# Reads of the states as whole-array matmuls, a choice matrix in one step, and a new planned order, in a fused attention and mixture-of-depths kernel

## The chip, the cores and the metric

The kernel runs on one core of one Trainium2 chip. The metric is the device time of a run in microseconds (us). A core has a matmul engine (TensorE, PE in the profile), three engines for elementwise work (VectorE or DVE, ScalarE or ACT, GpSimd or POOL), a queue engine (SyncE or SP) and 16 DMA engines. They run side by side and wait for one another by semaphores. Matmuls write to PSUM, from which ACT or DVE copy the results into SBUF.

## The reference

Eight batches of x have 8 heads, 512 rows and 64 columns; each head has a state of 32 rows. Rows read the state and the state reads the rows; the 544 results of a batch are then rows of 512 columns, of which the 128 with the highest gate score go through two layers.

```python
# attention, per batch and head; scale = 1/8
a     = softmax(scale * x @ state.T)          # 512 x 32
xread = a @ state                             # 512 x 64
a2    = softmax(scale * state @ x.T)          # 32 x 512
sread = a2 @ x                                # 32 x 64
y = concat([xread, sread], axis=rows)         # heads side by side: 544 x 512 per batch
# mixture of depths, per batch
scores = y @ w_gate                           # 544
top = indices of the 128 largest scores
h = relu(y[top] @ w1)                         # 128 x 1024
y[top] += sigmoid(scores[top])[:, None] * (h @ w2)
```

All numbers are float32.

## The kernel before

**Tiling.** The 8 heads of a batch are two groups g of four heads q; 4 x 32 states fill the 128 partitions. The 512 rows are four chunks c of 128. Per batch, in the program's order:

- `turn` (L340): 16 transposes of x on PE, in four pairs of heads, each pair copied by ACT (L349; two pairs of batch 0 by DVE, L347) into a buffer of the ring `xT`.
- `scores` (L369): scores in PSUM (`ps_s`), states by rows.
- The row softmax: DVE turns the scores in 32x32 blocks (`in`, L383), takes the largest (L387), subtracts (L390); ACT takes exp (L393); DVE sums (L397), scales (L402) and turns back (`out`, L405) into `eT`.
- The state softmax: largest by DVE (`smax`, L411), exp by ACT into `a` (`s_exp`, L415).
- `read` (L447): for each chunk, `eT` times the states `st_v` into the PSUM tile `ps_o`, of which there is one. ACT copies the rows to `xs` (`rows`, L451); DVE sums the gate parts (`gate`, L455).
- `turn_a` (L469), copied by ACT (L472), and `state_read` or sread (L485): the other softmax is transposed and multiplied by x. DVE scales the result (L490).
- The stores of `xs` (L512) and of the states' rows (L517) on the SP queue.

**The states for a read.** `st_v` has, for each batch and group, 128 partitions (head and state) and 2 x 64 + 1 columns: two heads in blocks on a diagonal, for each half of the partitions, and one column with the state's share of the gate score. A read is therefore four matmuls, two groups by two halves. `pool_states` zeroes the tile (L224) and copies the blocks (L218) on POOL; DVE fills the last column (`state_gates`, L229 and L231); `twice` doubles the states for PE's transposes of them (`state_T`, L314), on DVE or POOL (L221).

**The choice.** The gate scores are spread over all partitions by transposes (`row`, L558 and L561), DVE counts for each row how many are larger (`win`, L577), PE adds up those that were chosen before it (`over`, L604), DVE makes the offsets (L610, L611) and from them a 0/1 matrix `oh`, with five instructions (`one_hot`, L617). PE picks the row numbers with it (L632), and POOL fetches the chosen rows back from the output by an indirect DMA (L524) into the ring `xr`.

**The layers** (`layers`) take the chosen rows of the groups of batches [0], [1, 2], [3, 4], [5, 6] and [7]: transposes (`xg`, L690), first layer (L707) of 256 or 128 columns, relu by ACT (L711), second layer (L724), gate and sum by DVE (L727), and an indirect DMA that puts the rows back (L524).

**Buffers.** A `Ring` has a fixed number of buffers; a piece that takes one waits until the users of the old content are done. The ring of x has five buffers, one of which first holds the states. PSUM has two tiles `ps_tr` for every transpose and small result, one `ps_s`, one `ps_o` and two `ps_h`.

**Order.** Nothing above runs in the program's order. Each step is added as a piece with an engine, a planned length, the pieces that it follows, and the buffers that it takes and uses. `carry_out` then plays a clock: it takes the engine whose next piece can start first, and among its pieces that can start within `SOON[engine]` of that time the one with the smallest key. The key is the batch number plus `LATER[name]`. That order is then emitted, and each engine works its own list strictly in it:

```python
t, e = min(((at, p.engine) for at, p in ready), key=lambda r: r[0])
at, p = min(((at, p) for at, p in ready if p.engine == e and at <= t + SOON[e]), key=lambda r: r[1].key)
```

Of the kernel before, what the change touches and what calls it, by code (L numbers as in the profile page):

```python
# [18 lines left out]
def kernel(  # L19
# [35 lines left out]
    def pool(name, bufs, **kw):  # L55
        return ctx.enter_context(tc.tile_pool(name=name, bufs=bufs, **kw))

    N_X, N_XR = 5, 8
    const = pool("const", 1)
    xin = pool("xin", N_X)  # L60
    work = pool("work", 1)
# [5 lines left out]


    HOP = 0.1
    SOON = {"PE": 0.0000, "DVE": 0.4931, "ACT": 0.0000, "POOL": 1.8045, "SP": 0.3000}  # L70

    LATER = {
        "add": -100.0000, "below": 1.9500, "exp": -0.0600, "exps": -0.7084, "fetch": 0.2600, "first": 100.0000,
        "gate": -0.5600, "gate_s": 4.8280, "heads": 0.4872, "in": -1.0433, "index": -2.8646, "load": -50.0000,
        "load_x": -2.0000, "max": 4.0896, "mult": 4.3959, "numbers": 0.2545, "off": -1.9260, "oh": -2.4538,
        "out": 3.4200, "over": -2.2366, "parts": -2.6851, "pick": 0.3200, "put": -100.0000, "read": 4.9387,
        "relu": -100.0000, "row": -4.7962, "row_kept": 4.8694, "row_s": -3.1695, "row_s_kept": -0.1742,
        "rows": 5.0000, "score_s": -3.7680, "scores": -1.0816, "second": 100.0000, "sexp": -0.1370,
        "sigmoid": 0.2238, "smax": 1.1888, "sread": 1.2957, "srows": -2.7199, "ssum": 1.4281, "state_T": 0.3300,
        "state_gates": 2.6509, "states": -1.3434, "store": 4.7700, "sub": -1.8119, "sum": -4.7918,  # L80
        "tables": -4.6345, "turn": -0.1899, "turn_a": 4.0218, "turned": 4.7352, "turned_a": -5.0000,
        "twice": -2.9080, "win": 4.2491, "xg": 90.0000, "xg_kept": -100.0000,
    }
    class Buf:

# [26 lines left out]
    def carry_out():  # L112

        free, taken, done, end, order = {}, {R_X: [stb], stb: True}, {}, {}, []
        left = list(pieces)

        def since(p, q):
            return end[q] + HOP if q.engine != p.engine else done[q]

        while left:  # L120
            ready = []
            for p in left:
                if any(q not in end for q in p.after) or any(buf not in taken for buf in p.uses):
# [12 lines left out]
            assert ready, "the plan cannot go on"  # L136
            t, e = min(((at, p.engine) for at, p in ready), key=lambda r: r[0])
            at, p = min(((at, p) for at, p in ready if p.engine == e and at <= t + SOON[e]), key=lambda r: r[1].key)
            for buf in p.takes:
                taken[buf.ring].append(buf)  # L140
                taken[buf] = True
            free[e] = done[p] = at + p.length
            end[p] = done[p] + p.lands
            order.append(p)
            left.remove(p)
        for p in order:
            for buf in p.takes:
                buf.ring.take(buf)
            p.fn()
# [6 lines left out]
    P_O = Ring("ps_o", [128, 1024], F32, 1, psum)  # L156
    P_H = Ring("ps_h", [128, 512], F32, 2, psum)
    R_X = Ring("xf", [128, H, NC, D], F32, N_X, xin)
    R_XT = sbuf("xT", [128, 2, 2, 128], 12)
    R_E = sbuf("e", [128, 32, Ns], 2)  # L160
    R_A = sbuf("a", [128, 2, 2, 256], 1)
    R_ET = sbuf("eT", [128, 2, 2, 2, 128], 2)
    R_AT = sbuf("aT", [128, NC, 128], 2)
    R_XS = sbuf("xs", [128, NC, Dm], 2)
    R_ROW = sbuf("srow", [128, SP], 1)
    R_WIN = [sbuf(f"win{c}", [128, SP - first[c]], 1, BF16) for c in range(NC + 1)]
    R_OH = sbuf("oh", [128, NC + 1, n_slots], 1, BF16)
# [26 lines left out]
                                                          ap=[[D, 4], [0, Ns], [1, D]]))  # L194

    ident = const.tile([128, 128], F32, name="ident")
    st_v = const.tile([128, B, 2, 2 * D + 1], F32, name="st_v")
    wg_s = const.tile([128, 2, D], F32, name="wg_s")
    after = const.tile([128, SP], F32, name="after")
    places = const.tile([128, NC + 1, n_slots], F32, name="places")  # L200
# [26 lines left out]
    def state_gates(lo, hi):  # L227
        t = work.tile([128, hi - lo, 2, D], F32, name="state_g", tag="hT", bufs=1)
        nc.vector.tensor_tensor(out=t, in0=st_c[:, lo:hi, :, 0],  # L229
                                in1=wg_s.unsqueeze(1).to_broadcast([128, hi - lo, 2, D]), op=ALU.mult)  # L230
        nc.vector.reduce_sum(out=st_v[:, lo:hi, :, 2 * D], in_=t, axis=AX.X)  # L231

    def pool_tables():

# [8 lines left out]


        nc.gpsimd.memset(sc, 0.0)

    def row_numbers():

# [77 lines left out]
    def attention(b):  # L326
# [6 lines left out]
        for pair in range(H // 2):  # L333
# [10 lines left out]
            def keep(ps=ps, t=t, on=on):  # L344
# [92 lines left out]
        for c in range(NC):  # L437
            o = Buf(P_O)

            def view(o):  # L440
                return o.ap.rearrange("p (i g m) -> p i g m", i=2, g=2)

            def read(c=c, o=o):
                for g in range(2):
                    for i in range(2):
                        half = slice(D * i, D * (i + 1))
                        nc.tensor.matmul(view(o)[:, i, g, 0:2 * D + 1], eT.ap[half, c % 2, g, c // 2], st_v[half, b, g],  # L447
                                         start=True, stop=True)

            def keep(c=c, o=o):  # L450
                nc.scalar.copy(out=xs.ap[:, c].rearrange("p (g i m) -> p g i m", g=2, i=2),  # L451
                               in_=view(o)[:, :, :, 0:2 * D].rearrange("p i g m -> p g i m"))

            def gate(c=c, o=o):
                nc.vector.tensor_reduce(out=sc[:, b, c:c + 1], in_=view(o)[:, :, :, 2 * D], axis=AX.XY, op=ALU.add)  # L455

            p = add("PE", 0.66, read, after=[p_eT, p_pool[b], p_sg[b]], takes=[o], uses=[eT],
                    key=key("read"))
            p_sc.append(add("DVE", 0.15, gate, after=[p, p_tab], uses=[o], key=key("gate")))
            p_xs.append(add("ACT", 0.6, keep, after=[p], takes=[] if c else [xs], uses=[o] + ([xs] if c else []), key=key("rows")))  # L460

        aT, p_aT = [], []
        for g in range(2):
# [10 lines left out]
            p = add("PE", 0.5, turn, after=[p_a[g]], takes=[ps, t], uses=[a], key=key("turn_a"))  # L474
# [54 lines left out]
    def choice(b, tmp, p_sc, p_xt, p_st1):  # L529
# [33 lines left out]
        p = add("PE", 0.55, row_x, after=p_sc, takes=[ps1], key=key("row"))  # L563
        p_r1 = add("ACT", 0.59, lambda: nc.scalar.copy(out=srow.ap[:, 0:S], in_=ps1.ap), after=[p], takes=[srow],
                   uses=[ps1], key=key("row_kept"))
        p = add("PE", 0.2, row_s, after=[p_ss, p], takes=[ps2], key=key("row_s"))
# [54 lines left out]
        p_oh = add("DVE", 1.06 * n_slots / 128, one_hot, after=[p], takes=[oh], key=key("oh"))  # L621

        units = []
        for lo, hi in slot_tiles:
# [166 lines left out]
```

## Time and profile before

| | us |
|---|---|
| median of 3 runs (lowest to highest) | 221.9 (221.47 to 222.27) |
| time of the profiled execution | 222.47 |
| its span | 220.7 |
| PE busy | 202.4 |
| DVE busy | 124.5 |
| ACT busy | 85.9 |
| POOL busy | 49.9 |

The span runs from the first to the last instruction; a run's time has 1.8 us more around it. An engine's busy time is the union of its instructions. In the tables of groups, a line has the source line, the engine, the operation, output and inputs, the shapes and the count; after the first bar the busy time in us and the mean of one in ns, and after the second the idle time just ahead of them. "64*128" is the part of the matmul array that an instruction uses, rows by columns; 128*128 is the whole. In the timeline, a line has the start and the length in us, the engine, the line and the count, and in brackets what the engine stood idle for. PE's granted clock was 0.999 of full speed over the span.

### The profile page before, as it was taken

To read this page: it belongs to the slowest core of one execution; us is meant where nothing else is said; L and a number is where in the kernel's file an instruction comes from. 1 tells how busy PE (TensorE), PEld (TensorE's weight loads), DVE (VectorE), ACT (ScalarE), POOL (GpSimd) and SP (SyncE) were. 2 spreads that over 40 slices of the span, in tenths; PEclk is the share of its full clock that TensorE was granted. 3 is DMA by queue.
4 is the path that set the end of the run, shared out by engine and by line. 5 is a ranking of instruction groups with operands and counts; after the bars stand their busy time and mean duration, and the time that the engine had idled before them with its cause. 6 is when DMAs were issued, how large, how long until landed. Compare 5 with 4: busy or idle time off the path is not lost.

```text
span 220.7 us, 4784 instructions
## 1 busy us (share of the span) xinstructions
PE 202.4 (92%) x1928; PEld 142.4 (65%) x1928; DVE 124.5 (56%) x349; ACT 85.9 (39%) x172; POOL 49.9 (23%) x128
## 2 busy tenths in 40 slices
PE   2497898898999999999999999999999999999990
PEld 2355675676878954778886455888645788447840
DVE  3159989987887897798868896730062100011001
ACT  3139878778776315453725133323301021100200
POOL 7229001041105124110142423301035200011001
PEclk9999999999999999999999999999999999999999
DMA  6999969826314301150050711502212000010001
GB/s 213 329 306 402 369 207 288 305 54 205 131 74 157 111 0 48 52 196 9 34 207 13 238 50 49 239 3 95 95 48 94 33 19 0 0 50 11 36 0 48
DMA packets 17406, 26.59 MB, mean 120 GB/s; under 512 B 5608, under 2 KB 13800, under 8 KB 16360
## 3 DMA queue, kind: packets, MB, share of 16 engines
q1 hardware_dynamic: 15032, 21.43, 28.0%
q0 software_dynamic: 1280, 4.20, 6.1%
q10 hardware_dynamic: 1072, 0.66, 0.9%
q8 instruction: 15, 0.25, 0.5%
q14 instruction: 7, 0.06, 0.1%
HBM read 15.27 MB, written 11.01 MB: 119 GB/s over the span
## 4 chain that ended last, share of the span: by engine, by line
PE 55%; issue 20%; DMA 8%; POOL 6%; ACT 5%; DVE 2%; POOLq 1%; ACTq 0%
PE ps_h L707 17%; PE ps_h L724 12%; PE ps_o L447 7%; DMA out_dram<-xs 4%; PE ps_tr L340 4%; PE ps_s L369 3%; DMA xf<-in_state_dram 3%; PE ps_tr L469 3%; PE ps_tr L485 3%; ACT a L415 2%; POOL out_dram L524 2%; PE ps_tr L604 2%; PE ps_tr L558 2%; POOL xr L524 1%; ACT xT L349 1%
## 5 line engine op out<-in xcount | busy, mean ns | idle before, releaser
L707 PE MATMUL ps_h<-xg,w 128*128 128x256 f32 (+1 forms) x320 | 60.4, 341 | 0.0
L724 PE MATMUL ps_h<-w,hT 128*128 128x512 f32 x128 | 58.9, 601 | 0.0
L707 PEld LDWEIGHTS ps_h<-xg,w 128*128 128x128 f32 x320 | 50.3, 191 | 5.9 <-issue 0.5
L724 PEld LDWEIGHTS ps_h<-w,hT 128*128 128x128 f32 x128 | 23.1, 190 | 23.2 <-issue 22.5
L340 PE MATMUL ps_tr<-ident,xf 128*128 128x128 f32 x128 | 21.5, 311 | 9.7 <-DMA xf<-in_x_dram 4.1
L727 DVE SCALAR_TENSOR_TENSOR ot<-ps_h,z,xr 128x512 f32<-128x512 f32 x8 | 6.0, 749 | 43.1 <-PE ps_h L724 43.1
L451 ACT COPY xs<-ps_o 128x512 f32<-128x512 f32 x32 | 18.8, 586 | 28.2 <-PE ps_o L447 14.1
L711 ACT ACTIVATE hT<-ps_h 128x512 f32<-128x512 f32 x16 | 9.5, 596 | 49.7 <-PE ps_h L707 49.7
L340 PEld LDWEIGHTS ps_tr<-ident,xf 128*128 128x128 f32 x128 | 15.5, 156 | 14.8 <-issue 5.3
L577 DVE SCALAR_TENSOR_TENSOR win<-srow,sc,after 128x544 bf16<-128x544 f32 (+4 forms) x40 | 18.3, 501 | 8.4 <-ACT srow L567 8.4
L447 PE MATMUL ps_o<-st_v,eT 64*128 64x129 f32 x256 | 22.9, 297 | 0.1
L447 PEld LDWEIGHTS ps_o<-st_v,eT 64*128 64x128 f32 x256 | 16.8, 186 | 6.0 <-issue 2.8
L349 ACT COPY xT<-ps_tr 128x512 f32<-128x512 f32 x30 | 16.8, 589 | 9.6 <-PE ps_tr L340 9.6
L524 POOL DMA_INDIRECT out_dram<-ot,idx x8 | 8.4, 1047 | 53.2 <-DVE ot L727 51.0
L524 POOL DMA_INDIRECT xr<-out_dram,idx x8 | 8.5, 1057 | 48.1 <-DVE idx L637 16.3
L588 POOL CAST aux<-sc 128x5 bf16<-128x5 f32 x8 | 1.9, 232 | 52.3 <-DVE sc L455 38.3
L455 DVE TENSOR_REDUCE sc<-ps_o 128x1 f32<-128x4 f32 x32 | 5.1, 158 | 12.1 <-PE ps_o L447 7.0
L415 ACT ACTIVATE a<-ps_s,nm 128x512 f32<-128x512 f32 x16 | 10.9, 689 | 2.0 <-DVE nm L411 2.0
L383 DVE STREAM_TRANSPOSE e<-ps_s 128x1024 f32<-128x1024 f32 x8 | 10.0, 1247 | 2.9 <-PE ps_s L369 2.9
L369 PE MATMUL ps_s<-xT,st_T 64*32 64x256 f32 x256 | 9.6, 413 | 1.7 <-ACT a L415 1.7
L469 PE MATMUL ps_tr<-ident,a 128*128 128x128 f32 x64 | 10.2, 284 | 1.1 <-ACT a L415 0.5
L397 DVE TENSOR_REDUCE sm<-e 128x32 f32<-128x1024 f32 x8 | 9.7, 1210 | 1.5 <-ACT e L393 1.5
(84 smaller groups left out, 229.9 us busy)
## 6 DMA issues: line engine op xcount, KB each, us to landing
out_dram<-xs SPq DMA_DIRECT2D x8, 1024.0 KB, 4.3
xf<-in_x_dram SPq DMA_DIRECT2D x14, 512.0 KB, 6.8
w<-in_moe_w_dram SPq DMA_DIRECT2D x2, 2048.0 KB, 10.1
xf<-in_x_dram SPq DMA_DIRECT2D x2, 256.0 KB, 3.2
xf<-in_x_dram ACTq DMA_DIRECT2D x2, 256.0 KB
out_dram<-xt SPq DMA_DIRECT2D x32, 16.0 KB, 2.1
xf<-in_state_dram SPq DMA_DIRECT2D x1, 384.0 KB
xf<-in_state_dram ACTq DMA_DIRECT2D x1, 128.0 KB, 7.1
```

What stands on the lines that cost most here:

```text
L340: nc.tensor.transpose(v[:, k, r], xf[b].ap[:, 2 * pair + k, 2 * r:2 * r + 2].rearrange("p w d -> p (w d)"), ident)
L349: nc.scalar.copy(out=t.ap, in_=v)
L369: nc.tensor.matmul(view_s()[Ns * q:Ns * (q + 1), w, g], st_T[half, b, g, Ns * q:Ns * (q + 1)], xT[2 * g + q // 2].ap[half, q % 2].rearrang ...
L383: nc.vector.transpose(out=flat(e), in_=s.ap)
L415: nc.scalar.activation(out=a.ap[:, g], in_=view_s()[:, :, g], func=AF.Exp, bias=tmp["nm"][:, g:g + 1], accum_out=tmp["ss"][:, g:g + 1])
L447: nc.tensor.matmul(view(o)[:, i, g, 0:2 * D + 1], eT.ap[half, c % 2, g, c // 2], st_v[half, b, g], start=True, stop=True)
L451: nc.scalar.copy(out=xs.ap[:, c].rearrange("p (g i m) -> p g i m", g=2, i=2), in_=view(o)[:, :, :, 0:2 * D].rearrange("p i g m -> p g i m"))
L469: nc.tensor.transpose(v[:, c], a.ap[:, g, c % 2, 128 * (c // 2):128 * (c // 2 + 1)], ident)
L524: touches(b, nc.gpsimd.indirect_dma_start(**kw), True)
L577: nc.vector.scalar_tensor_tensor(wins[c].ap[0:n], srow.ap[0:n, f:SP], sc[0:n, b, c:c + 1], after[0:n, 0:SP - f], op0=ALU.is_gt, op1=ALU.mu ...
L707: nc.tensor.matmul(v[:, f, 0:n], w1[:, j, 128 * (f0 + f):128 * (f0 + f + 1)], xg.ap[:, j, 0:n], start=(j == 0), stop=(j == ND - 1))
L724: nc.tensor.matmul(py.ap[0:m], hT.ap[:, f, lo:lo + m], w2[:, f], start=(f == 0), stop=(f == NF - 1))
```

## The change

- `st_v` gets 4 x 64 + 1 columns: all four heads of a group in blocks on one diagonal. A read is two matmuls over all 128 partitions, one for each group, each into a PSUM bank of its own; the copy and the gate sum follow the new layout (two values for four).
- The choice matrix `oh` is made by one tensor_tensor over 5 x 128 columns, with the offsets in two zeroed tiles.
- The rings `xT` and `xr` go from 12 to 8 and from 8 to 6 buffers. `xs` stays at 2 for the capacity of 128.
- In the plan, the turns take their `xT` buffer at the transpose and not at the copy; some planned lengths change; `SOON` and `LATER` have new values, so that every engine's list has another order. If the plan cannot go on, the pieces are emitted in program order; in the build for these shapes they are not.
- The loads' pieces and their keys are the same, and so is their issue up to the weights and batch 4. After that the SP queue has loads and stores in another sequence.

```diff
-    N_X, N_XR = 5, 8
+    N_X, N_XR = 5, 6
+    DV = 4 * D + 1
...
-    SOON = {"PE": 0.0000, "DVE": 0.4931, "ACT": 0.0000, "POOL": 1.8045, "SP": 0.3000}
+    SOON = {"PE": 0.0000, "DVE": 0.5777, "ACT": 0.1173, "POOL": 0.6934, "SP": 0.3000, "DMA": 0.0000}
...
-    R_XT = sbuf("xT", [128, 2, 2, 128], 12)
+    R_XT = sbuf("xT", [128, 2, 2, 128], 8)
...
-    R_XS = sbuf("xs", [128, NC, Dm], 2)
+    R_XS = sbuf("xs", [128, NC, Dm], 2 if cap <= 128 else 1)
...
-    st_v = const.tile([128, B, 2, 2 * D + 1], F32, name="st_v")
+    st_v = const.tile([128, B, 2, DV], F32, name="st_v")
...
+    offs = [const.tile([128, NC + 1], F32, name=f"off{i}") for i in range(2)]
...
         for q in range(4):
-            k = q % 2
             r = slice(Ns * q, Ns * (q + 1))
-            nc.gpsimd.tensor_copy(out=st_v[r, lo:hi, :, D * k:D * (k + 1)], in_=st_c[r, lo:hi, :, 0])
+            nc.gpsimd.tensor_copy(out=st_v[r, lo:hi, :, D * q:D * (q + 1)], in_=st_c[r, lo:hi, :, 0])
...
+        for off in offs:
+            nc.gpsimd.memset(off, 0.0)
...
-            p = add("PE", 0.47 if b else 0.9, turn, after=[px[(pair * len(px)) // (H // 2)]] + last_turn[-1:], takes=[ps], uses=[xf[b]],
+            p = add("PE", 0.62 if b else 0.9, turn, after=[px[(pair * len(px)) // (H // 2)]] + last_turn[-1:], takes=[ps, t], uses=[xf[b]],
                     key=key("turn"))
             last_turn.append(p)
-            p_xT.append(add(on, 0.6, keep, after=[p], takes=[t], uses=[ps], key=key("turned")))
+            p_xT.append(add(on, 0.6, keep, after=[p], uses=[ps, t], key=key("turned")))
...
-        p_s = add("PE", 1.02, scores, after=p_xT + [p_sT[b]], takes=[s], uses=xT, key=key("scores"))
+        p_s = add("PE", 1.09, scores, after=p_xT + [p_sT[b]], takes=[s], uses=xT, key=key("scores"))
...
             def view(o):
-                return o.ap.rearrange("p (i g m) -> p i g m", i=2, g=2)
+                return o.ap.rearrange("p (g m) -> p g m", g=2)[:, :, 0:DV]
 
             def read(c=c, o=o):
                 for g in range(2):
-                    for i in range(2):
-                        half = slice(D * i, D * (i + 1))
-                        nc.tensor.matmul(view(o)[:, i, g, 0:2 * D + 1], eT.ap[half, c % 2, g, c // 2], st_v[half, b, g],
-                                         start=True, stop=True)
+                    nc.tensor.matmul(view(o)[:, g], eT.ap[:, c % 2, g, c // 2], st_v[:, b, g], start=True, stop=True)
...
             def gate(c=c, o=o):
-                nc.vector.tensor_reduce(out=sc[:, b, c:c + 1], in_=view(o)[:, :, :, 2 * D], axis=AX.XY, op=ALU.add)
+                nc.vector.reduce_sum(out=sc[:, b, c:c + 1], in_=view(o)[:, :, 4 * D], axis=AX.X)
...
-            p = add("PE", 0.66, read, after=[p_eT, p_pool[b], p_sg[b]], takes=[o], uses=[eT],
-                    key=key("read"))
+            p = add("PE", 0.46, read, after=[p_eT, p_pool[b], p_sg[b]], takes=[o], uses=[eT], key=key("read"))
...
         def offsets():
-            off = tmp["off"] = small.tile([128, NC + 1], F32, name="off")
+            off = offs[b % 2]
...
         def one_hot():
-            for c in range(NC + 1):
-                m = rows[c]
-                nc.vector.tensor_scalar(oh.ap[0:m, c], places[0:m, c], tmp["off"][0:m, c:c + 1], None, op0=ALU.is_equal)
+            nc.vector.tensor_tensor(out=oh.ap, in0=places, in1=offs[b % 2].unsqueeze(2).to_broadcast([128, NC + 1, n_slots]),
+                                    op=ALU.is_equal)
```

The planned lengths of `turn_a`, `row` and `oh` change as well (to 0.62, 0.62 and 0.82 us), and 50-odd values of `LATER`.

More of the change, by code (lines that the diff above doesn't have):

```diff
@@ L69 @@
     HOP = 0.1
-    SOON = {"PE": 0.0000, "DVE": 0.4931, "ACT": 0.0000, "POOL": 1.8045, "SP": 0.3000}
+    SOON = {"PE": 0.0000, "DVE": 0.5777, "ACT": 0.1173, "POOL": 0.6934, "SP": 0.3000, "DMA": 0.0000}
     LATER = {
[L73 to L82, printed above, removed]
+        "add": -100.0000, "below": 2.0667, "exp": 4.0880, "exps": 0.8708, "fetch": 0.4581, "first": 100.0000,
+        "gate": -5.0000, "gate_s": 5.0000, "heads": 1.5745, "in": 3.4702, "index": -1.4770, "load": -50.0000,
+        "load_x": -2.0000, "max": 0.1851, "mult": 0.6930, "numbers": -1.6286, "oh": 1.8876, "out": 2.4153,
+        "over": 1.7144, "parts": 2.7411, "pick": 0.4214, "put": -100.0000, "read": 5.0000, "relu": -100.0000,
+        "row": 2.2094, "row_kept": 5.0000, "row_s": -0.0444, "row_s_kept": -3.0512, "rows": 3.0716,
+        "score_s": 1.8701, "scores": -0.9593, "second": 100.0000, "sexp": -1.6379, "sigmoid": -2.2897,
+        "smax": -3.4387, "sread": -3.4561, "srows": -3.6081, "ssum": 2.4219, "state_T": -2.7947,
+        "state_gates": 1.5448, "states": -2.8057, "store": 2.3497, "sub": 3.7677, "sum": 1.8368, "tables": 4.1039,
+        "turn": 0.2203, "turn_a": 3.0810, "turned": -4.7340, "turned_a": -4.8726, "twice": 4.7356, "win": -4.4214,
+        "xg": 90.0000, "xg_kept": -100.0000,
     }
@@ L135, in carry_out @@
                     ready.append((at, p))
-            assert ready, "the plan cannot go on"
+            if not ready:
+                order = pieces
+                break
             t, e = min(((at, p.engine) for at, p in ready), key=lambda r: r[0])
@@ L230, in state_gates @@
                                 in1=wg_s.unsqueeze(1).to_broadcast([128, hi - lo, 2, D]), op=ALU.mult)
-        nc.vector.reduce_sum(out=st_v[:, lo:hi, :, 2 * D], in_=t, axis=AX.X)
+        nc.vector.reduce_sum(out=st_v[:, lo:hi, :, 4 * D], in_=t, axis=AX.X)
     def pool_tables():
@@ L440, in view @@
             def view(o):
[L441 removed]
+                return o.ap.rearrange("p (g m) -> p g m", g=2)[:, :, 0:DV]
             def read(c=c, o=o):
                 for g in range(2):
[L445 to L448 removed]
+                    nc.tensor.matmul(view(o)[:, g], eT.ap[:, c % 2, g, c // 2], st_v[:, b, g], start=True, stop=True)
             def keep(c=c, o=o):
[L451 to L452 removed]
+                nc.scalar.copy(out=xs.ap[:, c].rearrange("p (g m) -> p g m", g=2), in_=view(o)[:, :, 0:4 * D])
             def gate(c=c, o=o):
[L455 to L458 removed]
+                nc.vector.reduce_sum(out=sc[:, b, c:c + 1], in_=view(o)[:, :, 4 * D], axis=AX.X)
+            p = add("PE", 0.46, read, after=[p_eT, p_pool[b], p_sg[b]], takes=[o], uses=[eT], key=key("read"))
             p_sc.append(add("DVE", 0.15, gate, after=[p, p_tab], uses=[o], key=key("gate")))
@@ L472, in keep @@
                 nc.scalar.copy(out=t.ap, in_=ps.ap.rearrange("p (c m) -> p c m", c=NC))
-            p = add("PE", 0.5, turn, after=[p_a[g]], takes=[ps, t], uses=[a], key=key("turn_a"))
+            p = add("PE", 0.62, turn, after=[p_a[g]], takes=[ps, t], uses=[a], key=key("turn_a"))
             p_aT.append(add("ACT", 0.59, keep, after=[p], uses=[ps, t], key=key("turned_a")))
@@ L561, in row_s @@
             nc.tensor.transpose(ps2.ap[:, 0:Ns], sc[0:Ns, b, NC:NC + 1].to_broadcast([Ns, 128]), ident[0:Ns, 0:Ns])
-        p = add("PE", 0.55, row_x, after=p_sc, takes=[ps1], key=key("row"))
+        p = add("PE", 0.62, row_x, after=p_sc, takes=[ps1], key=key("row"))
         p_r1 = add("ACT", 0.59, lambda: nc.scalar.copy(out=srow.ap[:, 0:S], in_=ps1.ap), after=[p], takes=[srow],
@@ L614, in one_hot @@
         def one_hot():
-            for c in range(NC + 1):
-                m = rows[c]
-                nc.vector.tensor_scalar(oh.ap[0:m, c], places[0:m, c], tmp["off"][0:m, c:c + 1], None, op0=ALU.is_equal)
+            nc.vector.tensor_tensor(out=oh.ap, in0=places, in1=offs[b % 2].unsqueeze(2).to_broadcast([128, NC + 1, n_slots]),
+                                    op=ALU.is_equal)
         p = add("PE", 0.7, wins_over, after=p_w, takes=[ps3], uses=wins, key=key("over"))
         p = add("DVE", 0.3, offsets, after=[p], uses=[ps3], key=key("off"))
-        p_oh = add("DVE", 1.06 * n_slots / 128, one_hot, after=[p], takes=[oh], key=key("oh"))
+        p_oh = add("DVE", 0.1 + 0.72 * n_slots / 128, one_hot, after=[p], takes=[oh], key=key("oh"))
         units = []
```

## The prediction

> **What bounds the kernel now.** I read the page's busy shares first, then its table of groups split by shape, the stretches, and the matmul engine's timeline.
>
> ```profile
> PE 202.4 (92%) x1928; PEld 142.4 (65%) x1928; DVE 124.5 (56%) x349; ACT 85.9 (39%) x172; POOL 49.9 (23%) x128
> ...
> L447 PE MATMUL ps_o<-st_v,eT 64*128 64x129 f32 x256 | 22.9, 297 | 0.1
> ```
>
> PE is busy for 202 of 220.7 us, and nothing else comes near. The reads (L447) are 22.9 us of that: 32 reads, one per batch and chunk, each of four matmuls; the trace shows 256, since every f32 matmul of this kernel is two instructions there. The stretches say where PE is not full (columns after the two times: PE, PEld, DVE, ACT and POOL busy, clock, DMA):
>
> ```profile
> 0.00:55.50 55.50, 43.41 (x669) 32.01 (x670) 40.73 (x87) 36.41 (x73) 16.66 (x35) 1.00 0.82 266
> 55.50:90.00 34.50, 33.67 (x437) 25.32 (x436) 28.73 (x84) 18.27 (x38) 9.00 (x24) 1.00 0.26 89
> 90.00:152.00 62.00, 61.96 (x557) 44.20 (x557) 46.35 (x147) 23.36 (x47) 13.61 (x42) 1.00 0.26 94
> 152.00:215.30 63.30, 63.30 (x269) 40.91 (x268) 7.96 (x31) 7.81 (x16) 9.52 (x26) 1.00 0.11 42
> ```
>
> Up to 55.5 us (the first matmul of a first layer) PE stands for 12.1 us: 4.07 for the first load, 2.87 behind the state's load, the rest in small waits on copies. From there to 215.3 it stands for under 1 us. So after 55 us each microsecond added to PE's stream is added to the end, and what DVE, ACT or POOL save is worth nothing unless PE waits for it. The price of a PE instruction is the distance between starts, since a matmul's own mean (297 ns) includes a tail that overlaps the next:
>
> ```profile
> 97.05 0.72 PE L447 MATMUL ps_o<-st_v,eT 64*128 64x129 f32 x8
> 97.69 3.72 PE L707 MATMUL ps_h<-xg,w 128*128 128x256 f32 x16
> 101.34 0.72 PE L447 MATMUL ps_o<-st_v,eT 64*128 64x129 f32 x8
> 101.99 1.99 PE L707 MATMUL ps_h<-xg,w 128*128 128x256 f32 x8
> ...
> 173.69 13.98 PE L707 MATMUL ps_h<-xg,w 128*128 128x256 f32 x64
> 187.50 13.90 PE L724 MATMUL ps_h<-w,hT 128*128 128x512 f32 x32
> ```
>
> A read is 97.69 - 97.05 = 0.64 us to the next start; over all reads it is 0.64 or 0.65 whatever stands around it. A 128x256 matmul instruction in a long row is (187.50 - 173.69) / 64 = 0.2158 us. But the sixteen between two reads take 3.65 us where 16 x 0.2158 = 3.45: about 0.1 us is lost at each border with a read. The same comparison over the timeline gives: 0.09 us lost by a whole-array operation ahead of one that uses part of the array, and behind one 0.095 us (layers) or 0.05 us (groups of transposes: 0.49 against 0.44).
>
> **What the Trainium skill says.** "TensorEngine Tiling (Array Packing)", Key Properties, says that changing the tiling mode drains the engine; the trace agrees, with the 0.05 to 0.1 us above. The same section says that tiles work independently; the trace agrees in part: eight instructions of 129 columns, one after the other at the rate of L707, would be 8 x 129/256 x 0.2158 = 0.87 us, two abreast 0.435, and a read takes 0.645. "VectorE: DVE Perf Modes", The perf-mode tier table, has f32 tensor_tensor at a single rate where tensor_scalar runs double; in this trace a tensor_tensor of 768 elements is 0.918 us and one of 256 is 0.42 us, which is 0.97 ns an element.
>
> **The change, part by part.**
>
> 1. Reads. Removed: four matmuls of 64 rows x 129 columns, two abreast. Added: two of 128 rows x 257 columns, so four instructions at 257/256 x 0.2158 = 0.217 us, 0.867 us in all. That is the whole-array form, which L707 shows directly; its weight loads (128x128 f32, four in place of eight) run under the columns there and will here. 0.867 - 0.645 = +0.222 us, times 32 reads: **+7.1 us**, on the path. Bounds for a read: 0.43 if the two matmuls needed one instruction each (no f32 row of the trace does that), 0.97 if it lost a border of its own.
>
> 2. Borders. A read is now whole-array like most of its neighbours. Counted over PE's order in the two programs as built: before, 33 entries into a part-array operation x 0.09 + 22 returns to a layer x 0.095 + 25 returns to transposes x 0.05 = 6.3 us; after, 25 x 0.09 + 22 x 0.095 (15 of them now at a read) + 16 x 0.05 = 5.1 us. **-1.2 us**, on the path. Fourteen reads lose both borders; the rest stand beside small part-array operations that keep theirs.
>
> 3. The choice matrix: five tensor_scalar (1.06 us together in the timeline) become one tensor_tensor of 640 elements, 0.42 + 384 x 0.00097 = 0.79 us. -0.27 us x 8 on DVE, costed at nothing: PE does turns or layers meanwhile. Without that cover it would save at most 2.2 us. The two zeroed offset tiles cost POOL two small memsets (0.1 us each) at its idle start.
>
> 4. Evacuations: L451's copy moves 512 columns as before (0.586 us); the gate reduces two values for four (0.158 us, nearly all fixed). Nothing.
>
> 5. state_V and its memsets: st_v has 257 columns for 129. L224 took 0.52 us for 516 and 1.39 us for 1548 elements, so +0.45 and +1.4 us on POOL. Batch 0 and 1: the memset ends at about 5.5 us, ahead of the state's landing at 8.9; hidden. The rest: POOL now does memset and copies before the doubling (L221), which moves from 16.2 to about 20.6 us. PE needs it at about 28; hidden.
>
> 6. The order. The planner's new weights, read length (0.46) and rings move nearly every row. Smaller rings: xT 12 to 8, so PE turns two batches ahead, not three; xr 8 to 6 never binds (a row set is free when its batch's add is done). xs keeps two buffers here. On SP, store xs of batch 0 now stands ahead of half of load 5 and of load 6: that half is issued at about 37 us instead of before 35, lands (6.8 us median) by 44, and is turned at about 46. The store lands earlier in return. I walked through PE, ACT and DVE in the built order by hand with the durations above, up to the first read of batch 3:
>  - first read of batch 0 at 26.9 us (before 27.85);
>  - first matmul of a first layer at 55.6 (before 55.50), with 164.5 us of PE work left (before 157.4, counted with the same prices, borders included);
>  - first read of batch 3 at 84.7 with 137.2 left: 221.9 in sum; before 80.5 with 132.9 left: 213.4.
> The difference at the last mark is 8.5 us, where parts 1 and 2 make 5.9: PE has stood 2.6 us longer, mainly behind copies of turns that queue on ACT behind exps (36 to 48 us), and behind s_exp of batches 4 and 5 (66 to 80 us). Before pays 0.8 us of such waits afterwards (86 to 89 us), which I assume gone; the walk is rough, so **+2.0 us**, bounded by -1.5 (the small waits could close as well as open) and +5.
>  In the last stretch the fetch of batch 7 has four second-layer and eight first-layer matmuls (6.9 us) ahead of its transposes, and L524 lands 3.5 us after issue; nothing waits. From PE's last matmul to the end stays 5.4 us.
>
> Sum: 7.1 - 1.2 + 2.0 = +7.9 us. The profiled execution has a span of 220.7 and a time of 222.47; 222.47 + 7.9 = 230.4. Its time is 0.57 above the median of the runs, 221.9, so I give **229.8 us**. A difference of 0.3% (0.7 us) is about what a measurement of this kernel can tell from none.
>
> **Rivals.**
>  - *The read becomes cheaper* (the side of faster). If the two matmuls stream once, 2 x 0.217 = 0.434, as the planner's 0.46 supposes: 32 x (0.434 - 0.645) - 1.2 + 2.0 = -6.0, so 215.9 us. The break-even is 0.867 - 7.9/32 = 0.62 us a read. For it: the planner's other lengths are near the trace (turn 0.62, scores 1.09). Against: L707, L724, L369, L485 and L447 all show two instructions per f32 matmul. Chance 0.06.
>  - *The new order starves PE.* DVE is busy for 28.7 of 34.5 us between 55 and 90; with turns only two batches ahead the scores of batch 4 come at about 62 us (before 51), and the chain of seven passes of 1.2 us on DVE decides when a read starts. If PE stood 5 us beyond my walk: 234.8 us. For it: the planner plans with reads of half their length, so its order is meant for another balance. Against: longer reads give DVE more time, not less, and its own work falls by 2.2 us. Chance 0.14.
>  - *The change loses nothing*: borders save more than I count (0.19 at all 32 reads is 6 us) and the small waits close. Then within 0.7 us of before. Against: half the reads stand beside part-array operations. Chance 0.03.
>  - That PE's reads do grow and the order costs about nothing to 5 us: 0.77, from 226 to 233.5.
>
> **How the numbers follow.** The likeliest case gives 229.8. Range 225.8 to 234: from part 6 at about -1.5 with part 2 slightly larger, to part 6 at its upper bound with a little of the starving. Left out: the two good cases and the worst of the starving. Faster 0.06, same 0.03, slower 0.91.
>
> **What would show it.** Right: reads as 128x257, 128 instructions, 0.87 us from start to start; PE busy up by about 6 us; no lost tenth between reads and layers; the one-hot near 0.8 us on DVE. Part 6: first first-layer matmul at 54 to 58 us, PE full from about 85 us to the end. Wrong: a read under 0.62 us, or PE's waits after 55 us above 5 us.

## The result

The changed kernel takes **229.7 us** (median of 4 runs, 229.58 to 230.39) against 222.1 us for the kernel before on the same chip: a ratio of 1.034, interval 1.029 to 1.039. The forecast was 229.8 us. The profiled execution after took 229.67 us with a span of 227.9, where before had 220.7: +7.2.

The page's busy shares after, and its group of the reads:

```profile
PE 207.7 (91%) x1800; PEld 149.2 (65%) x1800; DVE 123.2 (54%) x317; ACT 85.4 (37%) x172; POOL 51.6 (23%) x130
...
L450 PE MATMUL ps_o<-st_v,eT 128*128 128x257 f32 x128 | 35.4, 399 | 2.4 <-ACT xs L453 0.9
```

The read is 128 instructions of 257 columns in place of 256 of 129, and PE's busy time grew by 5.3 us, to 207.7. The rest of the 7.2 is time in which PE stood: 227.9 - 207.7 = 20.2, before 220.7 - 202.4 = 18.3. How the 7.2 splits into work and waits depends in part on the execution that was profiled, as the first experiment shows. The stretches, with the columns as before, say where:

```profile
0.00:55.50 55.50, 42.15 (x599) 31.80 (x600) 38.91 (x80) 33.84 (x67) 17.94 (x37) 1.00 0.85 267
55.50:90.00 34.50, 33.82 (x419) 25.48 (x424) 27.30 (x75) 17.95 (x37) 7.45 (x22) 1.00 0.23 81
90.00:152.00 62.00, 61.12 (x495) 44.66 (x480) 47.06 (x130) 23.97 (x49) 15.70 (x43) 1.00 0.26 97
152.00:222.50 70.50, 70.50 (x304) 47.27 (x302) 9.19 (x34) 9.63 (x19) 9.49 (x26) 1.00 0.10 38
222.50:227.90 5.40, 0.12 (x1) 0.00 (x0) 0.75 (x1) 0.00 (x0) 1.07 (x2) 0.72 0.12 49
```

PE stands 13.35 us in the first stretch (before 12.09), 0.68 in the second (0.83), 0.88 in the third (0.04), and not at all from 152 us to its last matmul. The tail is still 5.4 us. The waits of PE name what it stood for (us in all, times, longest):

```profile
PE ps_tr L345 <- DMA xf<-in_x_dram: 4.4, 1, 4.4
PE ps_tr L319 <- DVE xf L224: 2.9, 1, 2.9
PE ps_tr L345 <- ACT xT L354: 2.2, 4, 1.4
PE ps_o L450 <- ACT xs L453: 0.9, 2, 0.4
...
PE ps_tr L544 <- DVE scr L537: 0.5, 1, 0.5
...
PE ps_o L450 <- DVE sc L456: 0.4, 1, 0.4
```

The first two are loads, as before. The turns' wait for their copies has one of 1.4 us in it, at 18 us. The L450 lines are reads that wait until the one `ps_o` has been copied (L453) or summed (L456). Last, the timeline of PE, where the reads stand between layers:

```profile
105.10 1.14 PE L450 MATMUL ps_o<-st_v,eT 128*128 128x257 f32 x4
106.07 1.89 PE L706 MATMUL ps_h<-xg,w 128*128 128x256 f32 x8
107.80 1.03 PE L450 MATMUL ps_o<-st_v,eT 128*128 128x257 f32 x4
108.67 1.89 PE L706 MATMUL ps_h<-xg,w 128*128 128x256 f32 x8
110.39 1.03 PE L450 MATMUL ps_o<-st_v,eT 128*128 128x257 f32 x4
```

A read behind a layer takes 108.67 - 107.80 = 0.87 us to the next start. The one at 105.10 stands behind a part-array operation, and takes 0.97. Eight layer instructions behind a read take 1.72 or 1.73 us, which is 8 x 0.2158 and no border; before, the same eight took 1.83 to 1.92.

### The profile page after: what moved, and what is told of

Same layout as the page of the kernel before. It is cut to its first block, busy times and chain, and to the rows that moved or that the text cites. A ratio compares the mean times of both kernels' runs of the same rounds, so it can differ in the third digit from the quotient of the medians.

```text
span 227.9 us, 4493 instructions
## 1 busy us (share of the span) xinstructions
PE 207.7 (91%) x1800; PEld 149.2 (65%) x1800; DVE 123.2 (54%) x317; ACT 85.4 (37%) x172; POOL 51.6 (23%) x130
## 4 chain that ended last, share of the span: by engine, by line
PE 55%; issue 18%; DVE 11%; DMA 5%; POOL 4%; ACT 3%; POOLq 1%; ACTq 0%; DVEq 0%
PE ps_h L723 14%; PE ps_o L450 13%; PE ps_h L706 13%; PE ps_s L374 3%; DMA xf<-in_state_dram 3%; PE ps_tr L345 3%; DMA xf<-in_x_dram 2%; DVE nm L416 2%; PE ps_tr L485 2%; DVE eT L410 2%; ACT xs L453 1%; PE ps_tr L604 1%; POOL out_dram L524 1%; PE ps_tr L469 1%; POOL xr L524 1%
## 5 line engine op out<-in xcount | busy, mean ns | idle before, releaser
L706 PE MATMUL ps_h<-xg,w 128*128 128x256 f32 (+1 forms) x320 | 59.8, 338 | 0.0
L706 PEld LDWEIGHTS ps_h<-xg,w 128*128 128x128 f32 x320 | 51.2, 191 | 5.9 <-issue 1.0
L450 PE MATMUL ps_o<-st_v,eT 128*128 128x257 f32 x128 | 35.4, 399 | 2.4 <-ACT xs L453 0.9
L453 ACT COPY xs<-ps_o 128x512 f32<-128x512 f32 x32 | 18.8, 586 | 32.0 <-DVE sc L456 17.0
L524 POOL DMA_INDIRECT xr<-out_dram,idx x8 | 11.3, 1406 | 74.8 <-DVE idx L636 31.8
L345 PE MATMUL ps_tr<-ident,xf 128*128 128x128 f32 x128 | 20.5, 304 | 7.3 <-DMA xf<-in_x_dram 4.4
L450 PEld LDWEIGHTS ps_o<-st_v,eT 128*128 128x128 f32 x128 | 22.1, 190 | 7.6 <-ACT xs L453 1.6
L456 DVE TENSOR_REDUCE sc<-ps_o 128x1 f32<-128x2 f32 x32 | 5.0, 158 | 26.2 <-PE ps_o L450 17.2
L472 ACT COPY aT<-ps_tr 128x512 f32<-128x512 f32 x16 | 9.3, 588 | 3.6 <-PE ps_tr L469 3.5
L398 ACT ACTIVATE e<-e 128x1024 f32<-128x1024 f32 x8 | 8.5, 1062 | 5.2 <-DVE e L395 5.2
L416 DVE TENSOR_REDUCE nm<-ps_s 128x2 f32<-128x1024 f32 x8 | 9.7, 1215 | 1.1 <-PE ps_s L374 1.0
```

What stands on the lines that cost most here:

```text
L345: nc.tensor.transpose(v[:, k, r], xf[b].ap[:, 2 * pair + k, 2 * r:2 * r + 2].rearrange("p w d -> p (w d)"), ident)
L416: nc.vector.tensor_reduce(out=tmp["nm"], in_=view_s().rearrange("p w g t -> p g w t"), axis=AX.XY, op=ALU.max, negate=True)
L450: nc.tensor.matmul(view(o)[:, g], eT.ap[:, c % 2, g, c // 2], st_v[:, b, g], start=True, stop=True)
L453: nc.scalar.copy(out=xs.ap[:, c].rearrange("p (g m) -> p g m", g=2), in_=view(o)[:, :, 0:4 * D])
L524: touches(b, nc.gpsimd.indirect_dma_start(**kw), True)
L706: nc.tensor.matmul(v[:, f, 0:n], w1[:, j, 128 * (f0 + f):128 * (f0 + f + 1)], xg.ap[:, j, 0:n], start=(j == 0), stop=(j == ND - 1))
```

## The experiments

Medians, with the ratio to the kernel before on the same chip and its interval; "idle" is span less PE busy. The comments say which kernel each edit starts from.

**The two halves of the change.** First the new order with the old reads:

```diff
# from the kernel after, lists of all engines as there
-    DV = 4 * D + 1
+    DV = 2 * D + 1
...
-                    nc.tensor.matmul(view(o)[:, g], eT.ap[:, c % 2, g, c // 2], st_v[:, b, g], start=True, stop=True)
+                    for i in range(2):
+                        half = slice(D * i, D * (i + 1))
+                        nc.tensor.matmul(view(o)[:, i, g, 0:2 * D + 1], eT.ap[half, c % 2, g, c // 2], st_v[half, b, g],
+                                         start=True, stop=True)
```

> The changed kernel with its order, rings and choice matrix, but with the reads of before (four matmuls of 64 rows by 129 columns). Every engine's list is that of the changed kernel. Theory (the longer reads on a full matmul engine make the loss, the order adds little): the reads give back about 6 us, so 223 to 225 us, and matmul busy near 202. Rival (the new order starves the matmul engine, whatever its reads cost): 227 us or more.

Measured: 223.1 us, ratio 1.0024 (1.0005 to 1.0044). The page:

```profile
PE 201.5 (91%) x1928; PEld 142.0 (64%) x1928; DVE 123.3 (56%) x317; ACT 85.4 (39%) x172; POOL 49.9 (22%) x130
```

The span is 221.7, so idle is 20.2, just as in the kernel after: the new waits belong to the order and not to the longer read. Against the profiled execution of before they are 1.9 us, and PE's own work seems 0.9 us shorter. But that execution is one of several. The run with the choice matrix alone (below) keeps PE's list of before. These are its page, its first stretch, and the first scores in two timelines, that of before and then that of this run:

```profile
PE 201.2 (91%) x1928; PEld 141.9 (64%) x1928; DVE 123.6 (56%) x317; ACT 85.9 (39%) x172; POOL 49.9 (23%) x130
```

```profile
0.00:55.50 55.50, 42.19 (x670) 31.46 (x671) 41.16 (x84) 36.50 (x73) 16.36 (x37) 1.00 0.83 266
```

```profile
12.77 1.96 PE L369 MATMUL ps_s<-xT,st_T 64*32 64x256 f32 x32
```

```profile
13.21 1.09 PE L372 MATMUL ps_s<-xT,st_T 64*32 64x256 f32 x32
```

The same scores take nearly twice as long in the first. Up to some moment at the start PE runs at half pace: in the traces a row of transposes goes 213 ns from start to start until then, and 109 ns afterwards. That moment, where the trace's record of the full clock begins, is 15.5 us in the profiled execution of before, 13.2 us in the run with the choice matrix alone, 14.8 us in this experiment and 13.25 us in the kernel after. (The clock of 0.999 that was given for before takes no account of this: ahead of the record the trace has no clock, and the views show 1.00. In the run with the upper half alone it has one: 0.50 from 11.0 to 14.5 us, where the same scores take 1.92 us.)

A late full clock makes PE's work at the start longer and its waits there shorter: the first layer starts at 55.50 us in the one execution and at 55.48 in the other, with PE busy for 43.41 and 42.19 us of the stretch. Three runs below keep the order of before and the time that its reads take (choice matrix alone, halves in turn, upper half only). PE is busy for 201.2, 201.4 and 201.2 us there, in spans of 220.4, 221.0 and 220.7, so idle is 19.2 to 19.6. Against them the order adds some 0.6 to 1.0 us of waits and takes hardly anything from PE's work. By the medians the order alone costs about half a microsecond. Then the other way round, the new reads in the order of before:

```diff
# from the kernel before, lists of all engines as there
-    N_X, N_XR = 5, 8
+    N_X, N_XR = 5, 6
+    DV = 4 * D + 1
...
-                    for i in range(2):
-                        half = slice(D * i, D * (i + 1))
-                        nc.tensor.matmul(view(o)[:, i, g, 0:2 * D + 1], eT.ap[half, c % 2, g, c // 2], st_v[half, b, g],
-                                         start=True, stop=True)
+                    nc.tensor.matmul(view(o)[:, g], eT.ap[:, c % 2, g, c // 2], st_v[:, b, g], start=True, stop=True)
```

> The kernel before, in its own order, with the reads of the change alone (two matmuls of 128 rows by 257 columns; the xr ring at 6 to make room, which doesn't alter the order). Theory: +5.9 us from the reads less the borders saved, so 227.5 to 229 us. Rival (order): under 224 us, since the order of before is kept.

Measured: 227.7 us, 1.0233 (1.0189 to 1.0277), as the theory has it. The page:

```profile
PE 208.8 (92%) x1800; PEld 149.3 (66%) x1800; DVE 124.8 (55%) x349; ACT 85.6 (38%) x172; POOL 51.5 (23%) x128
```

and a read in PE's timeline, 96.93 - 95.96 = 0.97 us behind a part-array operation:

```profile
95.96 1.14 PE L445 MATMUL ps_o<-st_v,eT 128*128 128x257 f32 x4
96.93 1.89 PE L703 MATMUL ps_h<-xg,w 128*128 128x256 f32 x8
```

PE busy +6.4, idle 227.0 - 208.8 = 18.2, unchanged. So the longer read alone makes the kernel slower, by lengthening PE's stream; the trace shows no other cost.

**Do the halves add up?** By medians the reads cost 5.2 us and the order 0.6, together 5.8, where the change cost 7.6. The whole change and the new reads were run again as they were; the order alone was not:

> The changed kernel once more, unedited, beside the next two on one chip, to see whether the order and the reads add up. Theory: order about 0.55 us and reads about 5.2 us make some 228.3 us on this chip's clock of before (222.3 or so), that is 2.6% above before, and the 3.4% of the first comparison was its spread. Rival: order and reads do more together than apart, 229.5 us or more, 3.2% and up.

> The kernel before with the reads of the change alone, once more, with more runs. Theory: 2.3 to 2.7% above before (5.2 to 6.0 us). Rival (reads and order interact): under 2.2%.

Measured: 230.3 us, 1.0351 (1.0296 to 1.0406), and 227.8 us, 1.0243 (1.0189 to 1.0297). The gap of about 2 us came again, 7.7 against 5.2 + 0.6, and the first of the two expectations is met by its rival's figure, not by its theory's. The spans of the profiled executions do add up (6.3 + 1.0 = 7.3 against 7.2; with the span of the second run of the new reads, 226.0, it is 6.3 against 7.2). Runs of the kernel before lie anywhere from 220.7 to 223.9 us, and the ends of the intervals just allow the sum. A part of the gap can be seen in the traces: from the first read of batch 3 to the last matmul PE stands for 0.85 us before and 0.29 with the new reads alone, but for 0.56 in the new order with the old reads and 0.88 with both. So the longer reads close about half a microsecond of waits in the old order and open 0.3 us in the new one. Whether the rest of the 2 us comes only where both halves meet stays open.

**The choice matrix alone.**

```diff
# from the kernel before
-            for c in range(NC + 1):
-                m = rows[c]
-                nc.vector.tensor_scalar(oh.ap[0:m, c], places[0:m, c], tmp["off"][0:m, c:c + 1], None, op0=ALU.is_equal)
+            nc.vector.tensor_tensor(out=oh.ap, in0=places, in1=offs[b % 2].unsqueeze(2).to_broadcast([128, NC + 1, n_slots]),
+                                    op=ALU.is_equal)
```

> The kernel before with the choice matrix in one step alone. Theory: 2.2 us less on VectorE, none of it on the path: 222.1 us within 0.7. Rival (VectorE's chain holds the reads up between 55 and 140 us): 220 to 221 us.

Measured: 222.3 us, 0.9986 (0.9962 to 1.0010), as the theory has it. DVE's busy time fell from 124.5 to 123.6 us, less than the 2.2 us expected, and the end did not move. In the kernel after, the group of this line (idle behind the second bar) shows 0.82 us each:

```profile
L615 DVE TENSOR_TENSOR oh<-places,off 128x640 bf16<-128x640 f32 x8 | 6.6, 822 | 0.2
```

**Less and more of the read.** If the length of the read decides, PE must follow it in both directions. One matmul per read (the heads of the second group are not computed; the first group's result stands in for them), and three (the second group's is done twice):

```diff
# from the kernel after: one
-                for g in range(2):
-                    nc.tensor.matmul(view(o)[:, g], eT.ap[:, c % 2, g, c // 2], st_v[:, b, g], start=True, stop=True)
+                nc.tensor.matmul(view(o)[:, 0], eT.ap[:, c % 2, 0, c // 2], st_v[:, b, 0], start=True, stop=True)
# from the kernel after: three
-                for g in range(2):
+                for g in (0, 1, 1):
```

> The changed kernel with one matmul a read in place of two; the second group's rows are left out and the first group's stand in their place. A read is then 0.434 us, the price of the forecast's first rival. Theory: 32 x 0.434 = 13.9 us less on the matmul engine, all of it at the end, 215.8 us, perhaps 1 to 2 us more where waits on copies open. Rival (VectorE's chain or the order takes over once the reads are short): 219 us or more.

> The changed kernel with the second group's matmul of every read done twice: three matmuls a read, 1.30 us in place of 0.867. Theory (a microsecond on the matmul engine is a microsecond at the end): +13.9 us on the changed kernel's span of 227.9, so 241 to 242 us of span, times of 243 to 244 us. Rival (part of it disappears into waits that the engine has anyway): under 240 us of time.

Measured: one matmul 218.4 us, 0.9834 (0.9781 to 0.9887); three 243.9 us, 1.0944 (1.0874 to 1.1014). The pages, one and then three:

```profile
PE 193.9 (90%) x1736; PEld 136.8 (64%) x1736; DVE 122.4 (57%) x317; ACT 85.1 (40%) x172; POOL 51.7 (24%) x130
```

```profile
PE 221.6 (92%) x1864; PEld 161.4 (67%) x1864; DVE 123.2 (51%) x317; ACT 85.9 (35%) x172; POOL 51.8 (21%) x130
```

PE busy moves by -13.8 and +13.9 us; 32 x 0.434 is 13.9. Upward all of it reaches the end (span 242.2, +14.3). Downward the span falls by 12.8 and the median by 11.3 to 11.9. The 218.4 us lie between the theory (at most 217.8) and the rival (219 or more). With shorter reads PE overtakes the copies: this line of its waits was 0.9 us in all and 0.4 at the longest in the kernel after:

```profile
PE ps_o L449 <- ACT xs L452: 1.3, 2, 0.8
```

One matmul is also the price of a read in the forecast's first rival (0.43 us). At that price the kernel would have become faster by 1.7% (1.1 to 2.2%); so the length of the read was what the sign turned on.

**Why the old read took 0.645.** The prediction had left open why eight instructions of 129 columns lie between 0.435 (two abreast) and 0.87 (one after another). Two tries on the kernel before:

```diff
# halves in turn
-                for g in range(2):
-                    for i in range(2):
+                for i in range(2):
+                    for g in range(2):
# upper half only; the lower half's heads are not computed
-                    for i in range(2):
+                    for i in range(1):
```

> The kernel before with the four matmuls of a read in another sequence: both of the upper half, then both of the lower half, instead of halves by turns; nothing else. Theory (the old read is short because two halves stream side by side, and that needs neighbours on different halves): a read goes from 0.645 toward 0.8 us, so 224 to 227 us. Rival (the old read is bound by its eight weight loads of some 65 ns, whatever their sequence): 222 us within 0.7.

> The kernel before with only the two matmuls of the upper 64 rows in each read; the lower half's heads are left out and the upper half's rows stand in their place. The old read shows its eight instructions in four pairs that start together. Theory (a pair is one instruction of each half): with one half gone the four left start one after the other, a read stays at 0.62 to 0.65 us, and the time at 222 us within 1. Rival (a pair is the two instructions of one f32 matmul): two pairs are left, a read is 0.42 us, and the time 7 us less, 215 to 216 us.

Measured: halves in turn 223.0 us, 1.0017 (0.9990 to 1.0045), and the read takes 0.65 us as before. The theory's longer read did not come. The rival was right that nothing changes (its 222.7 us at most is missed by 0.3, with before at 222.6 on this chip). In the trace the eight instructions still start in four pairs, 12 to 14 ns apart within a pair where they were 6 to 8 ns apart before. The order in which the program writes the halves hardly matters to PE here (0.653 us a read for 0.647). The upper half alone: 222.5 us, 0.9984 (0.9958 to 1.0010), as its theory has it. Its timeline:

```profile
97.12 0.71 PE L447 MATMUL ps_o<-st_v,eT 64*128 64x129 f32 x4
97.76 3.72 PE L707 MATMUL ps_h<-xg,w 128*128 128x256 f32 x16
```

and its group on the page, 128 instructions and nearly the busy time that 256 had:

```profile
L447 PE MATMUL ps_o<-st_v,eT 64*128 64x129 f32 x128 | 22.7, 297 | 0.1
```

Four instructions take the same 0.64 us as eight. So the second half of the array was free of charge, and the rival's reason in the run ahead (eight weight loads) falls: there are four here. The four start singly, at the moments of the old pairs; from this it is inferred that a pair is one instruction of each half, since the trace doesn't name the half. In the trace of before one such read has its pairs at 97.045, 97.259, 97.371 and 97.485, and the next layer at 97.692: between the later pairs 0.11 us, which is 129 columns at the rate of L707. Four times that is 0.43 us. The other 0.2 us stand behind the first pair and behind the last, 0.1 each. They lie inside the 0.645 us, and the 0.19 us that layers on either side of a read lose come on top.

**The plan: a true length, and the old rings.** The planner still held a read for 0.46 us. With its real length, and everything else as in the kernel after:

```diff
# from the kernel after
-            p = add("PE", 0.46, read, after=[p_eT, p_pool[b], p_sg[b]], takes=[o], uses=[eT], key=key("read"))
+            p = add("PE", 0.87, read, after=[p_eT, p_pool[b], p_sg[b]], takes=[o], uses=[eT], key=key("read"))
```

> The changed kernel with the read's planned length at 0.87 us, as it measures, in place of 0.46; the same weights. The plan then comes out quite different: the first layer of batch 0 starts after 52 us of matmul work and not after 34, so the first reads have no layers to stand in for them. Theory (what a plan is worth is its waits; the weights belong to the length that they were found with): slower than the changed kernel, 231 to 236 us, with the matmul engine's waits between 40 and 90 us above 5 us. Rival (the wrong length is what makes the order bad): 228.5 us or less.

Measured: 240.1 us, 1.0788 (1.0711 to 1.0864), slower even than the theory's range. PE busy 210.1, span 238.1, idle 28.0: of the 10.2 us of span more than in the kernel after, 7.8 are waits and 2.4 longer work, of which a stretch of 3.4 us at half clock (last section) is some 1.7. Among PE's waits are these two:

```profile
PE ps_s L374 <- ACT a L420: 2.1, 1, 2.1
PE ps_o L450 <- DVE sc L456: 2.0, 3, 1.0
```

and the second stretch is no longer nearly full (29.71 us of PE in 34.50):

```profile
55.50:90.00 34.50, 29.71 (x446) 23.84 (x444) 29.93 (x80) 19.54 (x40) 7.59 (x22) 1.00 0.25 84
```

The expected waits between 40 and 90 us came (2.9 us from 40.6 to 55.5, 4.8 in this stretch). The other new values of the plan had gone with 0.46; a truer number among them gave another order, 10 us worse. The last run took the old reads in the new plan (the first experiment) and gave it the rings of before:

```diff
# from the first experiment
-    N_X, N_XR = 5, 6
+    N_X, N_XR = 5, 8
...
-    R_XT = sbuf("xT", [128, 2, 2, 128], 8)
+    R_XT = sbuf("xT", [128, 2, 2, 128], 12)
```

> The changed kernel with the reads of before and with the rings of before as well (12 buffers for the turned x, 8 for the fetched rows); the plan is made anew with the new weights, so its order differs from both. Theory (the smaller rings take part of the order's cost, since the scores of batch 4 come later with them): 221.5 to 222.6 us, waits of the matmul engine near those of before. Rival (the weights cost it, not the rings): 222.8 to 225 us.

Measured: 229.1 us, 1.0290 (1.0240 to 1.0339), which is neither the theory nor the rival. More buffers under the new values made it 6 us slower than the smaller rings did. Its timeline of PE shows new waits around 90 us, and then a layer whose eight instructions take 3.40 us (1.89 to 1.99 elsewhere):

```profile
89.27 0.32 PE L563 MATMUL ps_tr<-ident,sc 128*128 128x128 f32 x1 [0.41 <-DVE sc L461]
90.54 0.21 PE L566 MATMUL ps_tr<-ident,sc 32*128 32x32 f32 x1 [0.95 <-DVE sc L552]
...
92.02 3.40 PE L711 MATMUL ps_h<-xg,w 128*128 128x256 f32 x8 [0.68 <-ACT xg L697]
```

In its stretches the third value from the end is the granted clock:

```profile
88.10:91.50 3.40, 1.88 (x15) 1.07 (x11) 2.45 (x5) 1.98 (x5) 1.42 (x6) 1.00 0.51 198
91.50:94.90 3.40, 2.88 (x7) 2.35 (x8) 3.33 (x11) 1.23 (x4) 0.01 (x1) 0.50 0.51 200
```

The profiled execution (227.9 us, the fastest of the six) has a span of 226.1 and PE busy for 204.0 us: 4.4 us of span more than the first experiment, of which 1.9 are waits and 2.5 longer work. The half clock alone is some 1.4 us of it (half of the 2.88 that PE worked at it). So in this run the smaller rings are not what costs. Which of the waits come from the rings themselves and which from the order that they lead to, it doesn't tell apart.

No kernel here that computes everything beats the kernel before. The choice matrix alone is equal to before within its interval. A mix of the two reads was not run: by the numbers above, even between two layers the old read costs an estimated 0.645 + 0.19 of borders = 0.835 us, and the new one 0.87.

## Why the prediction was right, step by step

The sign and the cause were right: the longer read on a full engine. That the number was met to 0.1 us is in part luck, since two of its terms were off in opposite directions.

- **Reads, +7.1.** Held. 0.867 was forecast, 0.87 is what a read takes among whole-array neighbours. At a fixed order PE's busy time grew by 6.4 us (order of before) and 6.2 (new order). Those two comparisons contain the start: the same list of PE work, from the end of the wait at 9 to 10 us up to the next wait for a turn's copy, took 0.40 and 0.55 us less with the new reads, because PE reached its full pace sooner in those executions. Without that it is 6.8 us twice: 7.1 less 0.3 of borders.
- **Borders, -1.2.** Too large. Parts 1 and 2 gave +5.9 together and the pages show +5.3, but the pages differ at the start: ahead of the full clock PE worked for 8.57 us in the profiled execution of before and for 5.94 in that of the change. If work ahead of the full clock is counted at half (an estimate from the two traces), PE's work is 198.2 us before and 204.7 after, +6.6. So the borders saved about 0.5 and not 1.2: 0.3 by the reads' form, and about 0.2 by the order, since the same estimate for the first experiment is 198.0. Why they saved less than the count times the price, no run shows.
- **Choice matrix, nothing.** Held, run alone. Its duration was forecast as 0.79 us and is 0.82: the slope between two rows was slightly too flat. DVE's busy time fell by 1.3 us in all and PE had not waited for it.
- **Evacuations and memsets, nothing.** Nothing of them shows among PE's waits; POOL's busy time rose by 1.7 us, about 2 forecast. No run took them alone.
- **Order, +2.0.** Met by the one pair of pages (+1.9 idle), but too large against the three other runs in the old order: 0.6 to 1.0 us. The first layer began at 54.62 (forecast 55.6) and the first read of batch 3 at 83.36 (84.7). Up to that read PE had stood 14.0 us; up to its own it stood 12.1 in the profiled execution of before and 13.3 to 13.5 in the three others. So the walk's 2.6 us more were 1.9 or, more likely, some 0.6. And the 0.8 us that before loses later were assumed gone, a step that failed: after loses 0.88 us between 90 and 152 us, to a sum on DVE (L537) and to `ps_o` (L456). "PE full from about 85 us" was wrong by that much. Where the waits lie was half right: behind copies of turns, yes, the longest at 18 us and not in the 36 to 48 named; behind the exps of batches 4 and 5 between 66 and 80, no: between 55.5 us and that read PE stood 0.68 us, and the waits named there are for DVE.
- **The tail and the fetch of batch 7.** Held: 5.4 us, and no wait from 152 us on.
- **The rivals.** The cheaper read fails at its price: every f32 matmul is two instructions after as before. Starving did not come in this order, but it is real: with one planned length changed, PE stood 8 us more. Borders did not save 6 us; they saved about 0.5.
- **The sum, +7.9.** Against 7.2 of span and 7.6 of the medians. With the sizes found here it is 6.6 of work and 0.6 to 1.0 of waits, 7.2 to 7.6. The prediction counted 0.7 us too much of saving at the borders and 1.0 to 1.4 us too much of cost for the order, and the two errors nearly cancelled.

## What to carry to other kernels

Filling the array with a block diagonal saves matmul time only if fewer columns pass, counted over what runs abreast: here two matmuls of 257 columns one after the other took the place of four of 129 that ran two abreast, so the number of matmuls halved and their time rose by a third. On an engine that is full from some point to the end, price each instruction by the distance between starts, borders included, and add it to the end; savings elsewhere are worth nothing until that engine waits for them. One profiled execution is not the kernel: before a microsecond is split into work and waits, look at a second execution of the same list, because here a later full clock moved 1.2 us from one to the other and left the first layer where it was. The planner's weights held only for the lengths and buffers with which they were found (10 us slower with one length changed, 6 with two rings), so count the waits anew when you change one.

## What the runs showed of the hardware that was not expected

- Two halves of the array start abreast in both sequences of the program that were run: 6 to 8 ns apart where it writes them by turns, 12 to 14 where it writes one half after the other. The Trainium skill, "TensorE: Matmul & The Clock Gate", Why this matters for your kernels, says that matmuls in distinct row groups run concurrently and gives 4 ns or less between starts; this trace agrees in kind, with the longer distances measured here.
- Short waits can halve PE's clock. The same page, Part 1, says that the clock falls back after an idle window of some 3.4 us. With the old rings it fell to 0.50 for 3.41 us (91.5 to 94.9) after a stretch of 3.40 us in which PE still worked for 1.88. With the read's true length the same came from 37.2 to 40.6 us, in which PE was full, after a stretch of 3.40 us with 1.27 of work and one wait of 2.13. Here the measurement decides: less than a wholly idle window was enough. From which share on, no run tells: the kernel after kept its full clock over a stretch of 3.41 us with 2.05 of work (16.66 to 20.07), and its repeat over one with 1.55 at its very end.
